# Reordering the head of a sliding-window attention and gated FFN kernel: first query halves of batch 0 ahead of the FFN, second halves between its first products

## The chip, the core and the metric

The kernel runs on one core of a Trainium2 chip. The metric is the device time of one execution in microseconds (us); the median of several executions counts. The engines are TensorE (PE in the profile; PEld is its weight load), VectorE (DVE), ScalarE (ACT), GpSimd (POOL) and SyncE (SP), which issues most DMA loads. An engine takes its instructions in the order of the program and waits where a value or a buffer is not ready.

## The reference

Causal attention with a window of 128 positions and 4 sink positions, 4 batches of 8 heads, 768 positions, head size 64; its output, with the heads joined to 512 columns, goes through a gated feed-forward network (FFN) with 1536 hidden columns. All inputs and outputs are float32.

```python
scores = scale * np.matmul(q, k.transpose(0, 1, 3, 2))
keep = is_sink | in_window            # pos < 4, or 0 <= query - key < 128
a = softmax(np.where(keep, scores, -1e9))
x = np.matmul(a, v).transpose(0, 2, 1, 3).reshape(B * S, H * D)
return (np.maximum(x @ w_gate, 0.0) * (x @ w_val)) @ w_out
```

## The kernel before

The order on every engine is written out by hand; nothing is rescheduled. Attention is done in units of two heads: a batch has four, U0 to U3 are batch 0, U4 to U7 batch 1 and so on. A unit passes through these steps, which the prediction calls by the names of the functions:

- `load_k`, `load_q` (L91 to L95), `load_v` (L97): DMA loads from SP. Keys and queries have three buffers each (`kf`, `qf`); values come for two units at once as seven loads (tiles 0 to 6, `vf`).
- `cast_kq` (L117) and `cast_v` (L106): POOL makes bf16 copies (`kn`, `qn`, `vn`).
- `T(u)` (L201): twelve PE transposes (L206); ACT copies the keys in five pieces (L211 to L216, `kE`), DVE copies the queries (L213, `qT`).
- `Sg(u, g)`, here S: scores for one of three groups of query columns (L229) and their exponential on ACT (L233, into `ee`). In the head a mask bias is first added on PE (L225); later DVE multiplies by a mask instead (L235).
- `V(u, part)`: products with the values and with ones (L247) for one half of the queries, 384 columns; then DVE normalises: a transpose (L253), a reciprocal (L254), a transpose (L255) and a product (L257) that writes this half of `xT`, the FFN's input. Part 0 needs score groups 0 and 1 and value tiles 0 to 3, part 1 groups 1 and 2 and tiles 2 to 6.

The FFN of a batch is `F1(b, g, m)`, for query half g and hidden column tile m of 12 (four gate products L273 over the four units of `xT`, ACT's relu L276, four value products L278, DVE's product L280 into `hT`), and `F2(b, t)`, six row tiles of the output (L289, L291, L292). F1 of half g needs that half of all four units. F1 and F2 take their PSUM banks in rotation from four (`G`), T, S and V from two pairs (`PP`); in the head T and V use `G` as well.

FFN weights are loaded in float32 by `load_w` (L124) into three buffers `ws` and cast on POOL by `cast_w` (L133): first column tiles 0 and 1, then 2 and 3, then 4 to 7 and 8 to 11, gate and value weights each in a buffer of its own. `load_wo` and `cast_wo` do the same for the output weights.

The head (L295 to L342) does all of batch 0's attention. After it come 18 slots per batch: 12 with two F1 each and 6 with one F2 each. `before` hangs loads and casts in front of a slot (L363 to L371 for the first batch), `after` hangs the 14 steps of the next batch's attention behind slots (`events`, `places`, L380 to L386). In slots 0 to 3 the first eight F1 are half 0 and half 1 of tiles 0 to 3.

Of the kernel before, what the change touches and what calls it, by code (L numbers as in the profile page):

```python
# [20 lines left out]
def kernel(  # L21
# [12 lines left out]
    nc = tc.nc  # L34
# [6 lines left out]
    KO = d_model // 128  # L41
# [49 lines left out]
    def load_k(u, eng=nc.sync):  # L91
        eng.dma_start(out=kf[u.i % NF][:], in_=k[u.b, 2 * u.p:2 * u.p + 2].rearrange("h (p n) d -> p h (n d)", n=NR))  # L92

    def load_q(u, eng=nc.sync):
        eng.dma_start(out=qf[u.i % NF][:], in_=q[u.b, 2 * u.p:2 * u.p + 2].rearrange("h (p n) d -> p h (n d)", n=NR))  # L95

    def load_v(w, tiles):  # L97
        dst = vf[w % NVF]
        b, h0 = w // 2, 4 * (w % 2)
        src = v[b, h0]  # L100
        for j in tiles:
            n = 128 if j < 6 else 14
            nc.sync.dma_start(out=dst[0:n, j, :, :],  # L103
                              in_=bass.AP(src.tensor, src.offset + ROWS[j] * D, [[D, n], [S * D, 4], [1, D]]))

    def cast_v(w, j0, j1):  # L106
        src, dst = vf[w % NVF], vn[w % NVN]
        nc.gpsimd.tensor_copy(dst[:, j0:j1, :, :].rearrange("p j h d -> p (j h d)"),  # L108
                              src[:, j0:j1, :, :].rearrange("p j h d -> p (j h d)"))
        for j in (1, 3, 5):  # L110
            if j0 <= j < j1:
                nc.gpsimd.tensor_copy(dst[0:4, j, :, :], src[0:4, 0, :, :])
# [8 lines left out]
    wsn = [0]  # L121
    staged = {}

    def load_w(m0, m1):  # L124
        for w, dst in ((moe_w_gate, wg), (moe_w_val, wv)):
            st = ws[wsn[0] % NW]
            wsn[0] += 1
            n = (m1 - m0) * 128
            nc.sync.dma_start(out=st[:, 0:KO * n].rearrange("p (k n) -> p k n", n=n),
                              in_=w.rearrange("(ko ki) n -> ki ko n", ki=128)[:, :, m0 * 128:m1 * 128])  # L130
            staged[m0, dst is wv] = st

    def cast_w(m0, m1):  # L133
        n = (m1 - m0) * 128
        for m in range(m0, m1):
            for x, dst in enumerate((wg, wv)):
                st = staged[m0, x == 1]
                o = (m - m0) * 128
                nc.gpsimd.tensor_copy(dst[:, :, m * 128:(m + 1) * 128],
                                      st[:, 0:KO * n].rearrange("p (k n) -> p k n", n=n)[:, :, o:o + 128])  # L140

    def load_wo(c):
        st = ws[wsn[0] % NW]
# [150 lines left out]
    with tc.manual_schedule():  # L294
        load_k(U[0])  # L295
        load_q(U[0], nc.scalar)
        setup()
        for u in (1, 2):
            load_k(U[u])
            load_q(U[u])  # L300
            if u == 1:
                load_v(0, (0, 1, 2, 3))
        load_v(0, (4, 5, 6))
        cast_kq(U[0])
        T(U[0])
        Sg(U[0], 0, bias=True)
        Sg(U[0], 1, bias=True)
        cast_kq(U[1])
        load_k(U[3])
        load_q(U[3])  # L310
        load_v(1, range(7))
        load_w(0, 2)
        T(U[1])
        Sg(U[0], 2, bias=True)
        cast_v(0, 0, 4)
        V(U[0], 0)
        Sg(U[1], 0, bias=True)
        cast_kq(U[2])
        cast_v(0, 4, 7)
        V(U[0], 1)  # L320
        Sg(U[1], 1, bias=True)
        T(U[2])
        Sg(U[1], 2, bias=True)
        V(U[1], 0)
        Sg(U[2], 0, bias=True)
        cast_kq(U[3])
        V(U[1], 1)
        Sg(U[2], 1, bias=True)
        T(U[3])
        Sg(U[2], 2, bias=True)  # L330
        cast_v(1, 0, 4)
        V(U[2], 0)
        Sg(U[3], 0, bias=True)
        cast_v(1, 4, 7)
        cast_w(0, 2)
        load_w(2, 4)
        V(U[2], 1)
        Sg(U[3], 1, bias=True)
        V(U[3], 0)
        Sg(U[3], 2, bias=True)  # L340
        V(U[3], 1)
        head[0] = False  # L342

        def kq_in(i):
            load_k(U[i])
            load_q(U[i])

        def events(i):

            a, c = U[i], U[i + 1]  # L350
            return [lambda: T(a), lambda: (Sg(a, 0), Sg(a, 1)), lambda: T(c), lambda: (Sg(a, 2), Sg(c, 0)),
                    lambda: (V(a, 0), V(a, 1)), lambda: (Sg(c, 1), Sg(c, 2)), lambda: (V(c, 0), V(c, 1))]

        ffn = [[lambda b=b, m=m: (F1(b, 0, m), F1(b, 1, m)) for m in range(FM)] +
               [lambda b=b, t=t: F2(b, t, b == B - 1 and t == 5) for t in range(6)] for b in range(B)]
        ffn[0][0:4] = [lambda: (F1(0, 0, 0), F1(0, 0, 1)), lambda: (F1(0, 0, 2), F1(0, 0, 3)),
                       lambda: (F1(0, 1, 0), F1(0, 1, 1)), lambda: (F1(0, 1, 2), F1(0, 1, 3))]
        before = {}

        def at(s, f):  # L360
            before.setdefault(s, []).append(f)

        at(0, lambda: (cast_w(2, 4), kq_in(4), load_w(4, 8)))  # L363
        at(1, lambda: (cast_kq(U[4]), kq_in(5), load_v(2, range(7))))
        at(2, lambda: cast_w(4, 8))
        at(3, lambda: load_w(8, 12))
        at(5, lambda: (cast_kq(U[5]), cast_v(2, 0, 7), kq_in(6), kq_in(7), load_v(3, range(7))))
        at(6, lambda: (cast_w(8, 12), load_wo(0), load_wo(1), load_wo(2)))
        at(9, lambda: (cast_kq(U[6])))
        at(10, lambda: (cast_v(3, 0, 7), [cast_wo(c) for c in range(3)]))  # L370
        at(12, lambda: (cast_kq(U[7]),))  # L371
        for b in (2, 3):
            s = 18 * (b - 1)
            i = NP * b
            at(s - 5, lambda i=i: (kq_in(i), kq_in(i + 1), load_v(i // 2, range(7))))
            at(s - 2, lambda i=i: (cast_kq(U[i]), kq_in(i + 2)))
            at(s + 1, lambda i=i: (cast_kq(U[i + 1]), cast_v(i // 2, 0, 7), kq_in(i + 3), load_v(i // 2 + 1, range(7))))
            at(s + 7, lambda i=i: (cast_kq(U[i + 2]), cast_v(i // 2 + 1, 0, 7)))
            at(s + 9, lambda i=i: (cast_kq(U[i + 3]),))
        after = {}  # L380
        for b in range(1, B):
            ev = events(NP * b) + events(NP * b + 2)
            places = [3, 4, 5, 6, 7, 8, 10, 11, 12, 13, 14, 15, 16, 17] if b == 1 else \
                     [0, 1, 2, 3, 5, 6, 7, 9, 10, 11, 12, 14, 15, 16]
            for p, f in zip(places, ev):
                after.setdefault(18 * (b - 1) + p, []).append(f)  # L386
        s = 0
        for b in range(B):
            for f in ffn[b]:
                for x in before.get(s, []):  # L390
                    x()
                f()
                for x in after.get(s, []):
                    x()
                s += 1
# [35 lines left out]
```

## Time and profile before

| what | value |
|---|---|
| median of 3 runs | 267.61 us (267.42 to 269.18) |
| the profiled execution | 267.93 us, span of its instructions 266.2 us |
| busy, share of the span | PE 247.5 us (93%), DVE 155.9 (59%), ACT 120.5 (45%), POOL 73.7 (28%) |
| chain that ended last | PE 73%, DVE 17% |
| DMA | 35.05 MB, mean 132 GB/s, nearly all of it on SP's queue |
| first F1 product | 31.20 us after the start |

The span runs from the first to the last instruction; the rest of the time lies around it. The busy share of PE counts a matmul from its issue, so waits inside a row are in it. The chain is followed back from the last instruction through whatever released each step. The page draws the span as 40 slices of 6.65 us, each digit the busy share in tenths.

### The profile page before, as it was taken

To read this page: it belongs to the slowest core of one execution; us is meant where nothing else is said; L and a number is where in the kernel's file an instruction comes from. 1 tells how busy PE (TensorE), PEld (TensorE's weight loads), DVE (VectorE), ACT (ScalarE), POOL (GpSimd) and SP (SyncE) were. 2 spreads that over 40 slices of the span, in tenths; PEclk is the share of its full clock that TensorE was granted. 3 is DMA by queue.
4 is the path that set the end of the run, shared out by engine and by line. 5 is a ranking of instruction groups with operands and counts; after the bars stand their busy time and mean duration, and the time that the engine had idled before them with its cause. 6 is when DMAs were issued, how large, how long until landed. Compare 5 with 4: busy or idle time off the path is not lost.

```text
span 266.2 us, 5290 instructions
## 1 busy us (share of the span) xinstructions
PE 247.5 (93%) x2073; PEld 145.3 (55%) x2084; DVE 155.9 (59%) x297; ACT 120.5 (45%) x250; POOL 73.7 (28%) x107
## 2 busy tenths in 40 slices
PE   1989699999999889999999999999999999999995
PEld 0445466656555456656655566566655456666443
DVE  4379744797836567698544566598543574444100
ACT  2757336744363437552661437743563423333221
POOL 6676448976523227000003523300000000000000
PEclk9999999999999999999999999999999999999999
DMA  6996999997079690000019956000003120000122
GB/s 233 287 270 205 354 311 281 368 277 273 2 221 285 212 236 2 1 2 0 2 46 293 309 182 126 0 2 1 0 2 118 42 79 0 2 1 0 42 97 100
DMA packets 44040, 35.05 MB, mean 132 GB/s; under 512 B 26992, under 2 KB 37488, under 8 KB 44016
## 3 DMA queue, kind: packets, MB, share of 16 engines
q1 hardware_dynamic: 43600, 34.20, 42.8%
q10 hardware_dynamic: 416, 0.52, 0.6%
q8 instruction: 16, 0.26, 0.4%
q14 instruction: 8, 0.07, 0.1%
HBM read 28.43 MB, written 6.29 MB: 130 GB/s over the span
## 4 chain that ended last, share of the span: by engine, by line
PE 73%; DVE 17%; SPq 3%; issue 2%; DMA 2%; ACT 1%; POOL 0%; DVEq 0%; POOLq 0%; ACTq 0%
PE g L289 21%; PE g L278 20%; PE g L273 20%; DVE R L255 5%; DVE t L253 5%; PE pp L247 4%; DVE xT L257 4%; PE pp L229 3%; PE pp L206 3%; DVE r L254 2%; DMA vf<-in_v_dram 2%; SPq L103 2%; DVE hT L280 1%; PE g L247 1%; SPq L92 1%
## 5 line engine op out<-in xcount | busy, mean ns | idle before, releaser
L273 PE MATMUL g<-xT,wg 128*128 128x384 bf16 x384 | 78.6, 326 | 2.0 <-DVE xT L257 1.3
L278 PE MATMUL g<-xT,wv 128*128 128x384 bf16 x384 | 78.1, 326 | 1.0 <-DVE hT L280 1.0
L280 DVE TENSOR_TENSOR hT<-gs,g 128x384 bf16<-128x384 f32 x96 | 51.1, 550 | 42.5 <-PE g L278 33.5
L276 ACT ACTIVATE gs<-g 128x384 f32<-128x384 f32 x96 | 46.3, 494 | 62.4 <-DVE hT L280 25.7
L289 PE MATMUL g<-wo,hT 128*128 128x512 bf16 (+1 forms) x289 | 63.6, 370 | 1.1 <-issue 0.8
L278 PEld LDWEIGHTS <-wv 128*128 128x128 bf16 x384 | 37.5, 98 | 28.0 <-issue 3.5
L273 PEld LDWEIGHTS <-wg 128*128 128x128 bf16 x384 | 35.7, 98 | 24.5 <-issue 2.3
L233 ACT ACTIVATE ee<-pp 128x1010 bf16<-128x1010 f32 (+2 forms) x48 | 44.4, 965 | 9.2 <-PE pp L229 9.2
L289 PEld LDWEIGHTS <-hT 128*128 128x128 bf16 x300 | 28.2, 98 | 30.5 <-issue 0.8
L235 DVE TENSOR_TENSOR ee<-ee,msk 128x1010 bf16<-128x1010 bf16 (+2 forms) x36 | 27.0, 756 | 17.4 <-ACT ee L233 16.8
L291 ACT COPY ot<-g 128x512 f32<-128x512 f32 (+1 forms) x24 | 13.9, 577 | 44.3 <-PE g L289 41.3
L115 POOL CAST kn<-kf 128x768 bf16<-128x768 f32 x16 | 13.6, 848 | 62.4 <-DMA kf<-in_k_dram 48.7
L253 DVE STREAM_TRANSPOSE t<-pp 128x384 f32<-128x384 f32 x24 | 13.8, 577 | 13.1 <-PE pp L247 12.5
L255 DVE STREAM_TRANSPOSE R<-r 128x384 f32<-128x384 f32 x32 | 18.5, 578 | 1.1
L108 POOL CAST vn<-vf 128x1792 bf16<-128x1792 f32 (+2 forms) x10 | 14.3, 1425 | 16.7 <-DMA vf<-in_v_dram 16.7
L229 PE MATMUL pp<-qT,kE 64*128 64x255 bf16 (+4 forms) x224 | 16.4, 252 | 2.6 <-DVE xT L257 2.4
L247 PEld LDWEIGHTS <-vn 128*64 128x64 bf16 x288 | 12.5, 109 | 9.2 <-issue 6.9
L229 PEld LDWEIGHTS <-kE 64*128 64x128 bf16 x224 | 8.1, 94 | 15.9 <-issue 11.9
L213 DVE COPY qT<-pp 128x768 bf16<-128x768 bf16 x12 | 11.5, 957 | 6.6 <-ACT kE L212 6.6
L115 POOL CAST qn<-qf 128x768 bf16<-128x768 f32 x16 | 13.7, 859 | 2.1 <-DMA qf<-in_q_dram 2.1
L257 DVE TENSOR_TENSOR xT<-pp,R 128x384 bf16<-128x384 f32 x24 | 13.4, 557 | 0.8
L247 PEld LDWEIGHTS <-ones 128*64 128x64 bf16 x288 | 12.5, 111 | 0.0
(55 smaller groups left out, 156.0 us busy)
## 6 DMA issues: line engine op xcount, KB each, us to landing
kf<-in_k_dram SPq DMA_DIRECT2D x16, 384.0 KB, 4.9
vf<-in_v_dram SPq DMA_DIRECT2D x48, 128.0 KB, 5.4
out_dram<-ot SPq DMA_DIRECT2D x23, 256.0 KB, 2.0
qf<-in_q_dram SPq DMA_DIRECT2D x15, 384.0 KB, 5.1
ws<-in_moe_w_out_dram SPq DMA_DIRECT2D x3, 1024.0 KB
ws<-in_moe_w_gate_dram SPq DMA_DIRECT2D x2, 1024.0 KB, 5.9
ws<-in_moe_w_val_dram SPq DMA_DIRECT2D x2, 1024.0 KB, 8.0
ws<-in_moe_w_gate_dram SPq DMA_DIRECT2D x2, 512.0 KB, 5.8
```

Source lines behind the costliest of these rows:

```text
L115: copy(dst[:], src[:].rearrange("p h (n d) -> p n h d", d=64))
L229: nc.tensor.matmul(out=ps[:, h, c0:c1], lhsT=kE[t][64 * h:64 * h + 64, x0:x0 + 128], rhs=qT[t][64 * h:64 * h + 64, q0:q0 + c1 - c0], start ...
L233: nc.scalar.activation(x, ps[:, :, 0:n], Act.Exp, bias=0.0, scale=scale)
L235: nc.vector.tensor_tensor(x, x, msk[:, g, 0:n].unsqueeze(1).to_broadcast([128, 2, n]), op=Alu.mult)
L247: nc.tensor.matmul(out=(pv, pd)[which][64 * h:64 * h + 64, o0:o0 + c1 - c0], lhsT=lhs, rhs=ee[u.i % NE][:, g, h, c0:c1], start=i == 0, sto ...
L253: nc.vector.transpose(out=t1[:], in_=pd[:, 0:CUT])
L255: nc.vector.transpose(out=R[:].rearrange("p (c e) -> p c e", e=32), in_=r[:].unsqueeze(2).to_broadcast([128, CUT // 32, 32]))
L273: nc.tensor.matmul(out=gp[:, 0:n], lhsT=wg[:, ko, m * 128:(m + 1) * 128], rhs=x[:, ko, c], start=ko == 0, stop=ko == KO - 1)
L276: nc.scalar.activation(gs[:, 0:n], gp[:, 0:n], Act.Relu, bias=0.0, scale=1.0)
L278: nc.tensor.matmul(out=vp[:, 0:n], lhsT=wv[:, ko, m * 128:(m + 1) * 128], rhs=x[:, ko, c], start=ko == 0, stop=ko == KO - 1)
L280: nc.vector.tensor_tensor(hT[:, m, c], gs[:, 0:n], vp[:, 0:n], op=Alu.mult)
L289: nc.tensor.matmul(out=op[:, 0:c1 - c0], lhsT=hT[:, m, t * 128:(t + 1) * 128], rhs=wo[:, m, c0:c1], start=m == 0, stop=m == FM - 1)
```

## The change

In the head only the first query halves of batch 0 are finished: the order on PE becomes T and two score groups for each unit with V of part 0 behind, and groups 2 of U0 and U1. Groups 2 of U2 and U3 and the four V of part 1 go between the first F1. The first sixteen F1 are now half 0 of tiles 0 to 7 and then half 1 of tiles 0 to 7, two to a slot. Weights come in six pairs of column tiles, gate and value of a pair in one buffer. Value tiles 4 to 6 are loaded and cast behind the first pair of weights. Loads and casts are hung on other slots, and the last eight of batch 1's fourteen attention steps move one slot ahead (the first six stay).

```diff
+    def load_w(i):
+        st = ws[wsn[0] % NW]
+        wsn[0] += 1
+        for x, w in enumerate((moe_w_gate, moe_w_val)):
+            nc.sync.dma_start(out=st[:, 1024 * x:1024 * x + 1024].rearrange("p (k n) -> p k n", n=256),
+                              in_=w.rearrange("(ko ki) n -> ki ko n", ki=128)[:, :, i * 256:(i + 1) * 256])
+        staged[i] = st
...
-        for u in (1, 2):
-            load_k(U[u])
-            load_q(U[u])
-            if u == 1:
-                load_v(0, (0, 1, 2, 3))
-        load_v(0, (4, 5, 6))
+        load_k(U[1])
+        load_q(U[1])
+        load_v(0, (0, 1, 2, 3))
+        load_k(U[2])
+        load_q(U[2])
         cast_kq(U[0])
         T(U[0])
         Sg(U[0], 0, bias=True)
         Sg(U[0], 1, bias=True)
         cast_kq(U[1])
         load_k(U[3])
         load_q(U[3])
-        load_v(1, range(7))
-        load_w(0, 2)
+        load_v(1, (0, 1, 2, 3))
+        load_w(0)
+        load_v(0, (4, 5, 6))
+        load_v(1, (4, 5, 6))
+        load_w(1)
+        load_w(2)
         T(U[1])
+        Sg(U[1], 0, bias=True)
+        cast_v(0, 0, 4)
+        Sg(U[1], 1, bias=True)
+        cast_kq(U[2])
+        V(U[0], 0)
+        T(U[2])
+        Sg(U[2], 0, bias=True)
+        Sg(U[2], 1, bias=True)
+        cast_kq(U[3])
+        V(U[1], 0)
         Sg(U[0], 2, bias=True)
-        cast_v(0, 0, 4)
-        V(U[0], 0)
...
+        T(U[3])
+        Sg(U[3], 0, bias=True)
+        cast_v(1, 0, 4)
+        cast_w(0)
+        Sg(U[3], 1, bias=True)
+        V(U[2], 0)
+        Sg(U[1], 2, bias=True)
+        V(U[3], 0)
         cast_v(0, 4, 7)
...
         cast_v(1, 4, 7)
-        cast_w(0, 2)
-        load_w(2, 4)
...
+        cast_w(1)
+        load_w(3)
         head[0] = False
...
+        ffn[0][0:8] = [lambda g=g, m=m, x=x: (F1(0, g, m), [f() for f in x], F1(0, g, m + 1)) for g, m, x in (
+            (0, 0, [lambda: Sg(U[2], 2, bias=True), lambda: V(U[0], 1)]),
+            (0, 2, [lambda: Sg(U[3], 2, bias=True), lambda: V(U[1], 1)]),
+            (0, 4, [lambda: V(U[2], 1), lambda: V(U[3], 1)]),
+            (0, 6, []), (1, 0, []), (1, 2, []), (1, 4, []), (1, 6, []))]
...
-        at(0, lambda: (cast_w(2, 4), kq_in(4), load_w(4, 8)))
-        at(1, lambda: (cast_kq(U[4]), kq_in(5), load_v(2, range(7))))
-        at(2, lambda: cast_w(4, 8))
-        at(3, lambda: load_w(8, 12))
-        at(5, lambda: (cast_kq(U[5]), cast_v(2, 0, 7), kq_in(6), kq_in(7), load_v(3, range(7))))
-        at(6, lambda: (cast_w(8, 12), load_wo(0), load_wo(1), load_wo(2)))
-        at(9, lambda: (cast_kq(U[6])))
-        at(10, lambda: (cast_v(3, 0, 7), [cast_wo(c) for c in range(3)]))
-        at(12, lambda: (cast_kq(U[7]),))
+        at(0, lambda: (cast_w(2), load_w(4), kq_in(4)))
+        at(1, lambda: (load_w(5), kq_in(5), load_v(2, range(7))))
+        at(2, lambda: (cast_w(3), cast_kq(U[4])))
+        at(3, lambda: (cast_w(4), load_wo(0)))
+        at(4, lambda: (cast_kq(U[5]), kq_in(6), kq_in(7), load_v(3, range(7))))
+        at(5, lambda: cast_v(2, 0, 7))
+        at(6, lambda: (cast_w(5), load_wo(1), load_wo(2)))
+        at(8, lambda: (cast_kq(U[6])))
+        at(9, lambda: (cast_v(3, 0, 7), [cast_wo(c) for c in range(3)]))
+        at(11, lambda: (cast_kq(U[7]),))
...
-            places = [3, 4, 5, 6, 7, 8, 10, 11, 12, 13, 14, 15, 16, 17] if b == 1 else \
+            places = [3, 4, 5, 6, 7, 8, 9, 10, 11, 12, 13, 14, 15, 16] if b == 1 else \
```

## The prediction

> **What bounds the kernel now.** I read the page first, then the chain that ended last in order of time, then the timeline of the first 45 us, and the two-microsecond windows for the DMA rate. The page's slices say where TensorE (PE) is not full and where DMA is:
>
> ```profile
> PE   1989699999999889999999999999999999999995
> DMA  6996999997079690000019956000003120000122
> ```
>
> One slice is 6.65 us. From the sixth slice on PE shows nines with a few eights; the first five (to about 31 us) are the head, the attention of batch 0, and only there can an order of work free much PE time. In the head DMA is also near full. The chain, in order of time (start, length, what):
>
> ```profile
> 15.95 0.59 DVE t L253
> ...
> 17.52 0.56 DVE xT L257
> 18.07 0.86 DVE qT L213
> ...
> 31.20 0.81 PE g L273 x4
> ...
> 41.76 0.67 PE pp L206 x12
> ```
>
> The head is no queue of PE work: its chain goes through the normalisation on VectorE (DVE: L253, L254, L255, L257) and through the copy of transposed queries (qT) that stands behind it. FFN products begin at 31.20 and run on PE without a break to T(U4), whose first matmul the timeline has at 41.59. Head work on PE is 18.7 us by the rows below (four units of 4.68), and 25.3 us pass between the first transpose at 5.93 and 31.20. The timeline gives the durations:
>
> ```profile
> 6.70 0.82 PE L206 MATMUL g<-ident,qn 128*128 128x128 bf16 x6
> ...
> 10.39 0.51 PE L206 MATMUL g<-ident,kn 128*128 128x128 bf16 x6
> ...
> 12.25 0.24 ACT L216 COPY kE<-kE 128x12 bf16<-128x12 bf16 x1
> ...
> 23.07 0.62 POOL L139 CAST wv<-ws 128x512 bf16<-128x512 f32 x1 [0.99 <-DMA ws<-in_moe_w_val_dram]
> ```
>
> Six transposes take 0.82 us at first and 0.51 later; T(U1)'s keys, transposed from 10.39, are usable only after ScalarE (ACT) ends its five copies at 12.49; the first `wv` tiles are there at 23.0, eight microseconds before use. The second place is the border between batches:
>
> ```profile
> 76.39 0.67 PE pp L206 x12
> ...
> 96.54 0.67 PE pp L206 x12
> ...
> 133.96 0.67 PE pp L206 x12
> ...
> 157.64 0.67 PE pp L206 x12
> ```
>
> These are T(U7) and T(U8), then T(U11) and T(U12). Between the first two lie 20.15 us with 17.8 us of PE work: four F2 of 2.65 (24 matmuls took 5.29), two F1 of 1.30, T 0.67, two score groups of 0.52, two V pairs of 1.45; 2.3 us are idle, because V(U7) ends slot 17 and the next batch's first F1 waits for its normalisation. Between the second two lie 23.68 us with 23.1 us of work (six F2, the rest alike): 0.6 us idle.
>
> **The change, part by part: the head.** Per-step durations, all from the head's timeline rows: T 0.66 on PE; S of groups 0 and 1, bias 0.54 then scores 0.32; S of group 2, 0.45 and 0.28; V part 0 0.74, part 1 0.83; exp starts 0.43 after the scores and takes 1.02 (0.89 for group 2); T's five key copies 1.08 on ACT; a normalisation 2.05 on DVE, a second one queued behind it 1.96 later; qT copy 0.95; F1 1.30, its `hT` product 0.55. Up to T(U1) nothing differs. Then, engine by engine in the new order:
>
> ```
> S1.0 scores 12.53   key copies of T1 end 12.49; bias was done 11.6: 0.9 idle
> S1.1, V0.0  12.85 to 14.45;  T2 14.45 to 15.11
> DVE         V0.0 normalised 14.57 to 16.62, then qT of T2 to 17.48
> S2.0 scores 17.52   bias was done 15.65: 1.9 idle
> S2.1, V1.0, S0.2    to 20.16;  T3 to 20.82
> DVE         V1.0 normalised 19.56 to 21.61, then qT of T3 to 22.47
> S3.0 scores 22.51   bias was done 21.36: 1.15 idle
> S3.1, V2.0, S1.2, V3.0   to 25.89
> DVE         V2.0 normalised to 26.60, V3.0 from 26.51 to 28.57
> F1(0,0,0)   three gate products at 27.13 (bank read by L253), the fourth
>             at 28.6 (needs xT of U3): 1.2 and 1.0 idle; ends 29.42
> S2.2 30.14, V0.1 30.97, F1 m1 32.27, F1 m2 33.57, S3.2 34.29, V1.1 35.12,
> F1 m3 36.42, F1 m4 37.72, V2.1 38.55, V3.1 39.38, F1 m5 40.68, F1 m6 41.98 (ends)
> DVE         V2.1, V3.1 normalised 38.63 to 42.65, only then hT of m5 to 43.12
> F1 m7       val half waits for that bank: 42.63 to 43.14; ends 43.79 = T(U4)
> ```
>
> The same work lies ahead of T(U4) in both kernels (four units and eight F1), so the head term is 43.79 - 41.59 = +2.2 us. FFN does start earlier (28.4 if its early products are counted against 31.20), but 4.8 us of attention are still to do, and waits are opened: today T(u) is followed by work of another unit while its copies run, in the changed order by its own scores; and the last V in front is directly followed by the product that needs it, where today V(U3,1) lies between. Each of five waits rests on rows good to some 0.2 us: +1.2 to +3.2.
>
> **What is costed at nothing, and its cover.** In SP's queue the 14 `vf` loads become 4 + 4 in front and 3 + 3 behind the first weights; weights become twelve loads of 512 KB instead of four of 512 KB and four of 1 MB, four more issues of about 0.4 us on an engine with nothing else to do. In the built program each SP load also waits until the one eight places before it has landed; at the landings below that lets every load out 3 us or more before its turn. Latest landings, from today's rows: pair 0 no later than today's 23.0 (fewer bytes ahead of it), six `vf` loads 0.55 MB at the 289 GB/s of 20 to 22 us: 24.9, then 1.05 MB a pair at the 350 GB/s of 26 to 28 us: 27.9, 30.9, 33.9. GpSimd (POOL) casts a pair in four steps of 0.56, and stands behind two V casts (1.2 us each): ready by 25.4, 30.2, 33.2, 36.2, needed at 27.1, 32.3, 36.4, 40.7. Cover is 1.7 us at least; once it is gone each microsecond late is one microsecond. The wait for a free buffer moves also: pair 3 takes pair 0's buffer and stands on SP ahead of U4's loads; these land by 39.1 behind pair 4, are cast by 40.7, and T(U4) wants them at 43.8. U5 and `vf` of batch 1 are needed 6 and 13 us later still. Second-half `vn` tiles are cast by about 27, wanted at 30.1.
>
> The Trainium skill speaks against the smaller loads: DMA: Bandwidth & Descriptors, Rules for kernel authors, asks for 1 MiB per DMA or more. Its fit of 2.0 us plus bytes over 436 GB/s per DMA would make a pair 6.4 us if nothing overlapped, pair 3 ready at about 46 and the sum some 6 us larger (an estimate from that page). Today's rows have several loads in flight and 350 GB/s, so I keep nothing.
>
> **Slots of batch 1.** The first six events keep their slots; the last eight go one slot earlier. V(U5) comes two slots behind V(U4) instead of three. In the later batches it already does: T(U9) at 103.06 to T(U10) at 127.44 holds 1.6 us idle, T(U5) at 48.27 to T(U6) at 69.89 holds 1.4: +0.2, bounds -0.2 (DVE has room) and +0.6 (one more `hT` late by 0.55). V(U7) moves to slot 16, as in the later batches: 2.3 - 0.6 = -1.7, bounds -1.3 and -2.1. U6's and U7's loads keep their order and the `wo` casts still precede slot 12.
>
> **Sum.** +2.2 + 0.2 - 1.7 = +0.7 on the profiled execution's 267.93 (span 266.2 and 1.7 around it), 268.6. That execution is 0.3 above the median of the runs, 267.61, so the forecast for the median is 268.3; with the terms' bounds -1.1 to +2.5, 266.5 to 270.1.
>
> **Rivals.**
> The head costs nothing. If DVE took qT ahead of the normalisation's end, the waits at 17.5 and 22.5 would shrink by 0.9 and 0.3, and if the first F1 found U3's values 1 us sooner the head would be level: -1.5, so 266.1. For it: of the 25.3 us of today's head 6.6 are idle and could be won. Against: the built program's order has each qT behind the normalisation on DVE, which takes one instruction after the other.
>
> PE slows down in the new gaps (this one is slower). The rows show slow transposes, 0.82 for 0.51, until about 10 us, with the profile's granted clock full throughout, and quick ones after gaps of up to 0.9 us. If a gap of 1.9 us, or the 2.2 of 25.9 to 28.6 with its short work between, brings that back for the 4 us it lasted from 5.93, 2 us of work are lost: 270.3, and 272.3 if twice. It decides from the first gap above 0.9 us that is followed by slow matmuls.
> On this the Trainium skill (TensorE: Matmul & The Clock Gate, part 1) says that the clock falls to half after an idle window of about 3.4 us; by that rule no gap here is long enough and the sum is unchanged.
>
> Weights late. If the loads of 512 KB run at the 213 GB/s that 16 to 18 us shows, a pair takes 4.9 us, pair 3 lands at 39.6, is ready at 41.9 and the seventh F1 ends 1.2 us late: 269.5; with pair 2 and POOL late as well, 271.
>
> The border is not healed. If V(U7) in slot 16 is still late because DVE lags, the -1.7 is lost: 270.0.
>
> **How the numbers follow.** Forecast 0.50, head level 0.16, PE slow 0.16, weights late 0.08, border 0.10. A change of 1% (2.7 us) is about what a measurement of this kernel can tell from none: below 264.9 lies 0.06 (of the second case, if more of the idle 6.6 us is filled), above 270.3 lie 0.06, 0.10, 0.04 and 0.04 of the others, 0.24; 0.70 within. The range reaches down to the level head and up past one slow spell: 266.0 to 271.2; the likeliest case's own is 266.5 to 270.1.
>
> **What will show it.** Right: scores L229 near 17.5 and 22.5 behind qT, the first FFN product near 27 to 28.6, T(U4) near 43.8, no POOL cast of weights that PE waits for, T(U7) to T(U8) with under 1 us idle. Wrong: T(U4) before 42 (head), L273 rows of more than 0.2 us a matmul after 28 us (clock), PE released by L138 casts (weights), or a chain through DVE at the start of batch 1.

## The result

The changed kernel takes 270.99 us (median of 20 runs, 267.94 to 273.56), the kernel before 267.71 (20 runs, 267.31 to 269.61). The ratio is 1.0096, with an interval of 1.0076 to 1.0115: slower by one per cent. The forecast was 268.3 with a range of 266.0 to 271.2. So the range held, but the likeliest case's own range, 266.5 to 270.1, did not, and the median lies above 270.3, for which the prediction had given a chance of 0.24. (Medians are over all runs; the ratio leaves out runs over 1.5% above the fastest of their kernel, four of the 20 here.)

The profiled execution took 270.69 us, 269.0 of it the span. First its page, the slices that were shown of before:

```profile
PE   0877899997999999999999999999999999999995
DMA  6999998981019957000009958000002220000123
```

Three things differ from the page of before. PE's first five slices are 0, 8, 7, 7, 8 where they were 1, 9, 8, 9, 6: the head has more idle PE time than before. And a 7 stands in the tenth slice (60.5 to 67.3 us), in batch 1, where nothing but nines and eights stood. DMA has 1, 0, 1 in the tenth to twelfth slice where it had 7, 0, 7: batch 1's loads are done earlier. Now the gaps of the head, from the timeline of PE (start, length, engine, line, what; in brackets the idle time ahead and what ended it):

```profile
17.72 0.40 PE L229 MATMUL pp<-qT,kE 64*128 64x253 bf16 x4 [1.90 <-DVE qT L213]
...
22.71 0.39 PE L229 MATMUL pp<-qT,kE 64*128 64x253 bf16 x4 [1.08 <-DVE qT L213]
...
27.32 0.65 PE L273 MATMUL g<-xT,wg 128*128 128x384 bf16 x3 [1.20 <-DVE t L253]
28.86 0.32 PE L273 MATMUL g<-xT,wg 128*128 128x384 bf16 x1 [0.89 <-DVE xT L257]
```

These are four of the waits in the prediction's walk, released by the instructions it named, each 0.2 to 0.3 us later than it put them. The chain in order of time has T(U4), T(U7) and T(U8) at

```profile
44.38 0.67 PE pp L206 x12
...
78.26 0.67 PE pp L206 x12
...
99.36 0.67 PE pp L206 x12
```

With the first matmul of T(U4) at 44.22 (before: 41.59), the first F2 at 75.50 (70.40) and T(U8) at 99.20 (96.38), the 2.8 us between the two spans split into three. In this kernel one score pair of U6 (0.54 us) stands ahead of the first F2 instead of behind it, and is taken out of the second and third term:

| stretch | predicted | measured in the profile |
|---|---|---|
| head, to T(U4) | +2.2 | 44.22 - 41.59 = +2.6 |
| T(U4) to the first F2 | +0.2 | 31.28 - 0.54 - 28.81 = +1.9 |
| first F2 to T(U8), the border | -1.7 | 23.70 + 0.54 - 25.98 = -1.7 |
| T(U8) to the end | 0 | 169.8 - 169.8 = 0 |

The second row is where this profile went wrong. It is seen on three engines at once, in the timeline from 58 us:

```profile
59.02 5.95 POOL L152 CAST wo<-ws 128x1024 bf16<-128x1024 f32 x6
64.93 0.82 POOL L115 CAST kn<-kf 128x768 bf16<-128x768 f32 x1
65.70 0.82 POOL L115 CAST qn<-qf 128x768 bf16<-128x768 f32 x1
```

```profile
62.89 1.01 DVE L280 TENSOR_TENSOR hT<-gs,g 128x384 bf16<-128x384 f32 x2
63.81 3.74 DVE L235 TENSOR_TENSOR ee<-ee,msk 128x1014 bf16<-128x1014 bf16 x2
```

```profile
63.02 0.36 PE L229 MATMUL pp<-qT,kE 64*128 64x255 bf16 x6 [1.16 <-DVE xT L257]
67.11 0.25 PE L247 MATMUL pp<-ee,vn 128*64 128x134 bf16 x3 [0.69 <-DVE ee L235]
72.92 0.81 PE L278 MATMUL g<-xT,wv 128*128 128x384 bf16 x4 [0.47 <-DVE hT L280]
```

L235 multiplies the scores of a group by the mask; both operands lie in SBUF. Two such products take 1.27 us together where no cast runs (the last experiment); here they take 3.74, the first alone 3.25. GpSimd runs eight casts without a pause from 59.02 to 66.5, and the first product ends 0.54 us behind the last of them, its own length. The last three rows are PE's waits in this stretch, 2.32 us together; the kernel before has one there, of 0.62. The second is V(U5), waiting for the long product. The first, 1.16, is behind the normalisation of V(U4), which stands on DVE behind another mask product, U5's first, and that took 1.82 beside the `v` casts (55.91 to 59.07). In the experiments below, as long as the product ahead of it on DVE keeps its 0.59, this wait goes with the length of U5's first product: 0.35 or 0.36 where that takes 0.69, 1.08 at 1.76 and 1.30 at 1.98. The products of `hT` (L280, one operand in PSUM) under the same casts take what they always take, 0.55 us each (0.54 to 0.56 over the whole run). In the kernel before the `wo` loads landed later and the casts waited for them in between (three pauses), and its longest mask product is 1.42 us.

### The profile page after: what moved, and what is told of

The parts are those of the page before. It is cut to its first block, busy times and chain, and to the rows that moved or that the text cites. A ratio compares the mean times of both kernels' runs of the same rounds, so it can differ in the third digit from the quotient of the medians.

```text
span 269.0 us, 5302 instructions
## 1 busy us (share of the span) xinstructions
PE 247.6 (92%) x2084; PEld 145.2 (54%) x2084; DVE 159.6 (59%) x297; ACT 120.2 (45%) x250; POOL 72.0 (27%) x107
## 4 chain that ended last, share of the span: by engine, by line
PE 74%; DVE 19%; issue 2%; DMA 2%; ACT 1%; POOL 0%; DVEq 0%; ACTq 0%
PE g L289 21%; PE g L278 20%; PE g L273 19%; DVE R L255 5%; DVE t L253 5%; PE pp L229 4%; DVE xT L257 4%; PE pp L247 4%; PE pp L206 3%; DVE r L254 2%; DVE hT L280 2%; DMA kf<-in_k_dram 2%; DVE qT L213 1%; PE pp L225 1%; PE g L247 1%
## 5 line engine op out<-in xcount | busy, mean ns | idle before, releaser
L278 PE MATMUL g<-xT,wv 128*128 128x384 bf16 x384 | 78.1, 326 | 1.9 <-DVE hT L280 1.9
L280 DVE TENSOR_TENSOR hT<-gs,g 128x384 bf16<-128x384 f32 x96 | 50.9, 550 | 40.5 <-PE g L278 30.4
L276 ACT ACTIVATE gs<-g 128x384 f32<-128x384 f32 x96 | 46.2, 494 | 60.5 <-PE g L273 26.7
L289 PE MATMUL g<-wo,hT 128*128 128x512 bf16 (+1 forms) x300 | 65.1, 371 | 0.0
L278 PEld LDWEIGHTS <-wv 128*128 128x128 bf16 x384 | 37.5, 98 | 28.5 <-issue 2.8
L235 DVE TENSOR_TENSOR ee<-ee,msk 128x1010 bf16<-128x1010 bf16 (+2 forms) x36 | 31.3, 877 | 15.2 <-ACT ee L233 14.7
L253 DVE STREAM_TRANSPOSE t<-pp 128x384 f32<-128x384 f32 x28 | 16.2, 578 | 12.2 <-PE pp L247 11.8
L257 DVE TENSOR_TENSOR xT<-pp,R 128x384 bf16<-128x384 f32 x28 | 15.6, 558 | 1.0
L247 PE MATMUL pp<-ee,vn 128*64 128x255 bf16 (+8 forms) x256 | 14.2, 236 | 0.7 <-DVE ee L235 0.7
```

Of the source, the lines that this page charges most:

```text
L235: nc.vector.tensor_tensor(x, x, msk[:, g, 0:n].unsqueeze(1).to_broadcast([128, 2, n]), op=Alu.mult)
L247: nc.tensor.matmul(out=(pv, pd)[which][64 * h:64 * h + 64, o0:o0 + c1 - c0], lhsT=lhs, rhs=ee[u.i % NE][:, g, h, c0:c1], start=i == 0, sto ...
L253: nc.vector.transpose(out=t1[:], in_=pd[:, 0:CUT])
L276: nc.scalar.activation(gs[:, 0:n], gp[:, 0:n], Act.Relu, bias=0.0, scale=1.0)
L278: nc.tensor.matmul(out=vp[:, 0:n], lhsT=wv[:, ko, m * 128:(m + 1) * 128], rhs=x[:, ko, c], start=ko == 0, stop=ko == KO - 1)
L280: nc.vector.tensor_tensor(hT[:, m, c], gs[:, 0:n], vp[:, 0:n], op=Alu.mult)
```

## The experiments

A second thing is not in this profile. Each run comes with the mean clock that was granted to PE. Of the 20 runs of the changed kernel, 13 have a mean below 0.997, mostly 0.993 or 0.994, of the kernel before 2 of 76. The median of the 7 others is 269.44, of the 13 it is 271.05. None of the low runs of this kernel has a profile. So two theories were on the table for the missing 2.7 us: the mask products behind rows of casts, and a clock that falls after a gap of the new head. The prediction's other rivals are excluded by the profile: no PE wait is released by a cast of weights, the border gained its 1.7.

**The new places of batch 1 alone.**

```diff
 (the kernel before)
-            places = [3, 4, 5, 6, 7, 8, 10, 11, 12, 13, 14, 15, 16, 17] if b == 1 else \
+            places = [3, 4, 5, 6, 7, 8, 9, 10, 11, 12, 13, 14, 15, 16] if b == 1 else \
```

> The kernel before with one part of the change alone: the last eight attention steps of batch 1 one slot earlier. Theory (border): V(U7) in slot 16 leaves its normalisation covered, so T(U7) to T(U8) has under 1 us idle; 1.7 us gained there, and V(U5) two slots behind V(U4) costs 0.2: about 266.1 us, ratio 0.994. Rival (the step that was mis-sized is the slot move itself: masks and two normalisations of V(U4) and V(U5) crowd on VectorE whatever GpSimd does): 1.8 us are lost between T(U5) and the first F2, 267.7, ratio 1.000.

Measured 265.78 us (265.48 to 266.41), ratio 0.9934 (0.9920 to 0.9949). First F2 to T(U8) gained 1.74, T(U4) to the first F2 lost 0.44: the border's term and the slots' term, each within the bounds of the prediction. So the 1.9 of the changed kernel is not the two-slot distance of V(U5) from V(U4); that costs 0.4.

**T ahead of V.**

```diff
-        V(U[0], 0)
         T(U[2])
+        V(U[0], 0)
...
-        V(U[1], 0)
-        Sg(U[0], 2, bias=True)
         T(U[3])
+        V(U[1], 0)
+        Sg(U[0], 2, bias=True)
```

> The changed kernel with T(U2) ahead of V(U0,0) and T(U3) ahead of V(U1,0), nothing else. Theory (the head's loss is the copy of the queries behind the normalisation on VectorE): the scores of U2 start at 16.3 instead of 17.7 and those of U3 at 20.1 to 20.4 instead of 22.7, the first FFN product 2.2 us sooner, T(U4) near 42.1: 268.7 us, ratio to before 1.004. Rival (the head is paced by loads, casts or ScalarE): T(U4) stays near 44.3 and the time at 271, ratio 1.010 to 1.012.

Measured 267.07 (266.04 to 268.09), ratio 0.9979 (0.9963 to 0.9995); T(U4) at 42.26, 1.96 earlier than in the changed kernel, as expected. The qT copies are ahead of the normalisations on DVE, and the waits of 1.90 and 1.08 are gone. The time fell by twice as much as T(U4) did: one run of 12, not 13 of 20, had a clock below 0.997, and in the profile of this kernel the longest mask product of U4 and U5 was 1.64 and T(U4) to the first F2 29.51 (31.28 in the changed kernel). It gained from both other causes too.

**The `wo` casts held.** GpSimd copies two elements of U5's last masked group ahead of the last two `wo` casts, so they can't start before that product is done; one cast goes ahead of the `v` casts.

```diff
-        at(9, lambda: (cast_v(3, 0, 7), [cast_wo(c) for c in range(3)]))
+        at(8, lambda: (cast_wo(0), cast_v(3, 0, 7)))
+        at(9, lambda: (gp_copy(held[:], ee[U[5].i % NE][:, 2, 1, 405:407]), cast_wo(1), cast_wo(2)))
```

> The changed kernel with the output weights' casts kept off the mask products of batch 1: the first third is cast ahead of the value cast, the other two wait on GpSimd for the mask product of U5's last group (a copy of two elements reads it). Theory (a mask product, two operands in SBUF, is shut out while GpSimd runs its casts back to back): the mask product of 3.25 us falls to about 0.7, the wait of PE ahead of V(U5) goes, 1.5 to 1.9 us are gained: 269.2 us, ratio 1.004, and the runs lie closer together than 267.9 to 273.6. Rival (VectorE is simply crowded because V(U5) follows V(U4) sooner): nothing gained, 271, ratio 1.010.

Measured 269.93 (268.26 to 271.09), ratio 1.0086 (1.0056 to 1.0116). In its profile U5's products take 0.68 and 0.58 and T(U4) to the first F2 takes 29.69 instead of 31.28, the 1.6 that was expected. The median is only 1.1 lower, and runs with the same clock hardly differ: the three at full clock have a median of 269.26 (269.44 in the changed kernel), the three others 270.93 (271.05). So the hold shows what made that product long; that it wins time is not shown, and 270.99 may come from runs with a shorter product than the profiled one. Half of the runs had the low clock, the profiled one among them, and there it can be seen. Windows of this kernel, then one of the T-first kernel and of the changed kernel (stretch, its length, busy time and instructions of PE, PEld, DVE, ACT, POOL, then the granted clock and DMA):

```profile
15.62:19.03 3.41, 1.52 (x17) 0.80 (x15) 2.63 (x5) 1.35 (x7) 2.39 (x5) 1.00 1.06 323
19.03:22.44 3.41, 3.41 (x28) 1.53 (x28) 0.85 (x3) 1.92 (x2) 2.99 (x6) 0.50 1.13 264
22.44:25.85 3.41, 2.69 (x32) 1.30 (x30) 1.96 (x3) 2.66 (x7) 2.11 (x4) 1.00 0.82 256
```

```profile
24.55:27.96 3.41, 1.70 (x10) 0.87 (x9) 2.20 (x5) 0.49 (x1) 2.44 (x5) 1.00 0.96 309
27.96:31.37 3.41, 3.41 (x41) 2.27 (x40) 2.43 (x6) 1.35 (x2) 2.60 (x5) 1.00 1.09 384
```

```profile
26.83:30.24 3.41, 2.03 (x14) 0.99 (x15) 2.10 (x5) 0.49 (x1) 2.68 (x6) 1.00 1.06 365
```

The clock changes only at multiples of 3.41 us from one another, on a grid whose place differs from run to run. The window with the 1.89 us gap (1.52 busy) is followed by exactly one window at 0.50; the windows with 1.70 and 2.03 busy are followed by full clock.

**The gap ahead of the first FFN product filled.**

```diff
         V(U[3], 0)
...
+        Sg(U[2], 2, bias=True)
+        V(U[0], 1)
         head[0] = False
...
-            (0, 0, [lambda: Sg(U[2], 2, bias=True), lambda: V(U[0], 1)]),
+            (0, 0, []),
```

> The changed kernel with S(U2,2) and V(U0,1) moved from behind the first F1 to ahead of it, into the wait for the last normalisation. Theory (the 2.2 us in which PE waits between V(U3,0) and the fourth product of the first F1 is a loss of order alone): 1.55 us of PE work go into it, 1.2 to 1.5 us gained: 269.6 us, ratio 1.007. Rival (VectorE is what ends last there; one more normalisation ahead of hT gives the wait back at the next bank): at most 0.3 gained, 270.7, ratio 1.009.

Measured 268.63 (266.19 to 271.1), ratio 1.0001 (0.9970 to 1.0032); T(U4) 42.97, 1.25 earlier. Seven of 12 runs still have the low clock (268.35 to 271.1); the other five take 266.19 to 267.34. So the spell does not need the gap that was filled; the longest one left is that of 1.90 us.

**All three edits at once.** T first, filled gap and held casts, as above.

> The changed kernel with three edits at once: T(U2) ahead of V(U0,0) and T(U3) ahead of V(U1,0); S(U2,2) and V(U0,1) ahead of the first FFN product; two of the wo casts held until U5's last masked group, and one put ahead of batch 1's v casts. Theory (three separate losses: the gaps behind qT, the gap ahead of the first FFN product, the mask products that lie under the casts): T(U4) near 41.0 (44.22 less the 1.96 and the 1.25 that the two head edits gave alone), T(U4) to the first F2 29.5 to 30.0, time 264.5 to 265.5, under the 265.8 of the new places alone. Rival (the edits fill the same gap, or take the same loss away): no better than the 267.1 of the best of them.

Measured 266.72 (264.45 to 267.15), ratio 0.9936 (0.9907 to 0.9965). No run of 8 had the low clock, but the expected 264.5 to 265.5 was met in two runs only. In the profile T(U4) is at 40.96, as expected, but T(U4) to the first F2 takes 31.20, not 29.5 to 30.0: the `wo` cast that had been put in front now meets U4, and a product of U4 takes 3.12 us under it. Earlier work of PE had moved the products, and the cast that was harmless in one kernel was in the way in the next.

**The gaps of the head kept warm.**

```diff
-            for h in range(2):
+            for h in list(range(2)) * (1 + again):
...
-        Sg(U[2], 0, bias=True)
+        Sg(U[2], 0, bias=True, again=3)
...
-        Sg(U[3], 0, bias=True)
+        Sg(U[3], 0, bias=True, again=2)
```

> The changed kernel with the two bias matmuls of S(U2,0) issued four times and those of S(U3,0) three times (the same values written again, 1.6 and 1.1 us more of PE work inside the gaps of 1.90 and 1.08 us), nothing else. Theory (the long gap in front lets PE's clock fall for some microseconds in part of the executions): no matmul moves in the profile, T(U4) stays near 44.2, but no execution has the spell, the runs lie closer together, and the median falls from 271.0 to 269 to 269.7, with the mask products still long in some. Rival (the clock spells come from elsewhere, or the median of 271 is the mask products' alone): 270.5 to 271.3 with the same spread; 271.5 if the added matmuls delay the scores.

Measured 270.47 (267.94 to 274.2), ratio 1.0075 (1.0046 to 1.0104): the median missed the expectation and lies by the rival's 270.5, and 4 of 12 runs, the profiled one among them, had a low clock. The profile says where:

```profile
26.54:29.95 3.41, 1.32 (x19) 0.94 (x18) 3.12 (x7) 0.85 (x1) 2.73 (x5) 1.00 1.05 349
29.95:33.37 3.42, 3.42 (x21) 1.68 (x22) 0.56 (x1) 0.96 (x2) 3.03 (x7) 0.50 1.05 370
...
64.08:67.50 3.42, 1.63 (x17) 1.04 (x17) 3.32 (x8) 1.75 (x2) 3.42 (x5) 1.00 0.01 5
67.50:70.91 3.41, 3.41 (x12) 1.47 (x10) 2.83 (x3) 1.06 (x3) 1.33 (x2) 0.50 0.00 0
```

```profile
30.22 1.49 PE L278 MATMUL g<-xT,wv 128*128 128x384 bf16 x4
...
34.53 0.81 PE L278 MATMUL g<-xT,wv 128*128 128x384 bf16 x4
```

The gap of 1.90 no longer does it. The two gaps of 1.20 and 0.89 ahead of the first FFN product do, together: no single one is long, but one window holds both. The second spell follows on the mask products: two of them take 3.44 us together beside casts (from 58.03), V(U4)'s normalisation is late behind them, PE waits 1.56 us for it (to 66.36), and that window has 1.63 us of work. So here the lock-out sets off the clock. The four products of L278 take 1.49 in the spell, 0.81 outside.

**Warm and held.** The two edits before, together.

> The changed kernel with the repeated bias matmuls and with the held wo casts. If the forecast missed only these two things, this is the kernel that it described: 267.8 to 268.6, runs within about 0.7 us of each other, T(U4) near 44.1 and T(U4) to the first F2 near 29.7. If one of the two is not the cause, its part stays: 269.3 to 270 (the held casts alone gave 269.9).

Measured 270.0 (268.99 to 271.84), ratio 1.0093 (1.0062 to 1.0124), low clock in 2 of 6. The expectation failed, for reasons that the profile shows: the FFN gap is still there (spell from 30.22 to 33.64), and the `wo` cast in front meets the first product of U4, which takes 2.72.

**The `wo` casts cut into pieces.**

```diff
-        for i in range(2):
-            nc.gpsimd.tensor_copy(wo[:, 4 * c + 2 * i:4 * c + 2 * i + 2, :].rearrange("p k n -> p (k n)"),
-                                  st[:, 1024 * i:1024 * i + 1024])
+        for i in range(8):
+            nc.gpsimd.tensor_copy(wo[:, 4 * c + i // 2, 256 * (i % 2):256 * (i % 2) + 256],
+                                  st[:, 256 * i:256 * i + 256])
```

> The changed kernel with each wo cast of 1024 columns cut into four of 256 (24 casts instead of 6, the same elements), nothing else. If a VectorE product with two SBUF operands waits for the end of the one GpSimd cast that runs when it starts, no mask product lasts over 1.3 us, and some 1.5 us are won: 269.3. If it waits for a whole row of casts that stand back to back, the longest stays near 3 us, the casts take longer by their own fixed parts, and the time is 271 or more.

```profile
60.69 7.46 POOL L152 CAST wo<-ws 128x256 bf16<-128x256 f32 x19
```

```profile
63.75 1.38 DVE L235 TENSOR_TENSOR ee<-ee,msk 128x1014 bf16<-128x1014 bf16 x2
```

The two products lie in the middle of a row of short casts and take 1.38 together: no long wait here. The others, under `v` casts that were not cut, still take up to 2.20. The time is 273.52 (269.27 to 275.81), ratio 1.0103 (1.0051 to 1.0155). The profiled run and one other come to 269.3 and 269.4, as the first theory said. Three have a clock of 0.987 or 0.988, which two spells would give (the warm kernel's 0.987 had two); the sixth, 272.87 at full clock, is unexplained. As an edit it loses.

**The filled kernel with one bias pair repeated.** `again=1` for S(U2,0), and the fill: the gap of 1.90 is shortened by the 0.54 us of one pair and not closed.

> The filled kernel (S(U2,2) and V(U0,1) ahead of the first FFN product) with the two bias matmuls of S(U2,0) issued twice: 0.54 us of PE work more, so its gap of 1.90 us becomes 1.36 us and is not closed. Theory (PE's clock is set in windows of 3.41 us, and a window in which PE is idle for 1.8 us or more is followed by one at half speed): with the gap of 1.36 no window reaches 1.8 us, so none of the runs has a granted clock under 0.997, where 7 of 12 of the filled kernel had one, and the median falls from 268.6 to 266.8, the level of its undisturbed runs (266.2 to 267.3). Rival (any gap over about a microsecond can do it, or the spells are chance): a third or more of the runs still show 0.992 to 0.994, median 268 to 269.

Measured 268.05 (266.82 to 271.86), ratio 1.0019 (0.9984 to 1.0055). In the profile the gap is 1.47, in a window with no more idle time than that. One run of 12 had the low clock, where 7 of 12 had it: with a gap of 1.47 instead of 1.90 most of the spells are gone. Six runs are at 266.8 to 267.3, the expected level; five more are at 268.8 to 270.3 at full clock. These have no profile; a long mask product would fit, but it is not shown.

**All edits, and three holds on GpSimd.**

```diff
-        at(3, lambda: (cast_w(4), load_wo(0)))
+        at(3, lambda: load_wo(0))
...
-        at(5, lambda: cast_v(2, 0, 7))
+        at(5, lambda: (gp_copy(held[:, 0:2], ee[U[4].i % NE][:, 1, 1, 505:507]), cast_v(2, 0, 7), cast_w(4)))
...
-        at(9, lambda: (cast_v(3, 0, 7), [cast_wo(c) for c in range(3)]))
+        at(8, lambda: (gp_copy(held[:, 2:4], ee[U[5].i % NE][:, 0, 1, 503:505]), cast_v(3, 0, 7), cast_wo(0)))
+        at(9, lambda: (gp_copy(held[:, 4:6], ee[U[5].i % NE][:, 2, 1, 405:407]), cast_wo(1), cast_wo(2)))
```

> T(U2) and T(U3) ahead of the V, the filled gap, and three holds on GpSimd's queue by copies of two elements: batch 1's first v casts and the casts of the fifth weight pair wait for U4's second masked group, the second v casts and the first wo cast for U5's first group, the last two wo casts for U5's third. Theory (mask products under rows of dense casts are what was left): no product of U4 or U5 over 1.4 us, T(U4) to the first F2 30.2 or less, no clock spells, 264.0 to 264.8, the lowest of all. Rival (a hold makes something else late: vn for V(U4), weights for the ninth F1, or wo for the first F2): PE waits for a POOL cast there, 266 to 268.

Measured 269.28 (267.58 to 269.98), ratio 1.0046 (1.0022 to 1.0069). The holds moved `v`, weight and k/q casts into one row and put that row on U4's third product:

```profile
50.96 0.60 POOL L139 CAST wg<-ws 128x512 bf16<-128x512 f32 x1
...
53.72 0.60 POOL L139 CAST wv<-ws 128x512 bf16<-128x512 f32 x1
54.27 0.82 POOL L116 CAST kn<-kf 128x768 bf16<-128x768 f32 x1
55.04 1.17 POOL L116 CAST qn<-qf 128x768 bf16<-128x768 f32 x1
```

```profile
51.48 5.28 DVE L236 TENSOR_TENSOR ee<-ee,msk 128x814 bf16<-128x814 bf16 x2
```

```profile
55.59 0.36 PE L248 MATMUL pp<-ee,vn 128*64 128x255 bf16 x5 [1.21 <-DVE ee L236]
```

The first of the two products takes 4.05 us, the longest seen, and gets in only as the seventh cast ends, counted from the one that runs when it starts (50.96) to that of `kn`. That a product waits for one cast is thus too little, and it is not only the wide `wo` casts that do it. Yet such a row does not always shut a product out. The kernel with the new places alone has the same weight casts, back to back from 50.34 to 56.65, and the same product in their midst:

```profile
52.02 0.61 POOL L139 CAST wg<-ws 128x512 bf16<-128x512 f32 x1
52.57 0.97 POOL L139 CAST wv<-ws 128x512 bf16<-128x512 f32 x1
53.49 1.06 POOL L139 CAST wg<-ws 128x512 bf16<-128x512 f32 x1
```

```profile
52.49 0.59 DVE L235 TENSOR_TENSOR ee<-ee,msk 128x814 bf16<-128x814 bf16 x1
```

It takes 0.59, and the one behind it 0.69; there it is the casts beside them that are longer, 0.97 and 1.06 instead of 0.61. Eight of 12 runs have the low clock. The profiled one has not; the waits of PE behind the product (1.21 and 1.56 us) are the likely place, as the next experiment's profile has it there. The rival of the expectation did not come true (no PE wait behind a cast); the kernel was slower by the very mechanism it was to remove.

**The changed order with shorter gaps and the same holds.** One bias pair again, five gate products of the first F1 issued once more, and the holds of the run before.

```diff
-        for ko in range(KO):
+        for ko, end in [(0, 0), (1, 0), (2, 0), (1, 0), (2, 1)] * ((b, g, m) == (0, 0, 0)) + [(0, 0), (1, 0), (2, 0), (3, 1)]:
```

> The changed kernel, its order unchanged, with the two gaps shortened by repeated work and the same three holds on GpSimd: the bias matmuls of S(U2,0) twice (gap 1.90 to 1.36 us), and five gate products of the first F1 issued once more ahead of its four (gap 0.89 to about 0.1; they write what the four then write again). If lock-out and clock spells are all that the forecast missed, this runs as forecast: 267.7 to 268.7, no run with a granted clock under 0.997, the spread not over 1.6 us (the kernel before: 266.95 to 268.49), T(U4) 44.2 to 45.2. If a term of the head or of the slots was also wrong: 269.5 or more without any spell.

Measured 274.12 (272.1 to 274.27), ratio 1.0217 (1.0181 to 1.0254). T(U4) is at 45.06 and the head has no spell; but the holds bring their 4.06 us product here too, and in the profile the clock is halved from 67.27 to 70.69, after a window with 1.53 us of work that holds the 1.56 us wait behind that product (5 of 6 runs have the low clock). It was to be the kernel of the forecast, and because of these holds it says nothing on that.

**The holds put right.** T first, filled gap, and every row of casts placed where no mask product of U4 or U5 is due: the fifth weight pair back in its old place, the first `v` casts behind U4's second product, the sixth pair behind U5's first, `wo` behind U5's third, the second `v` casts behind U7's.

```diff
-        at(5, lambda: cast_v(2, 0, 7))
-        at(6, lambda: (cast_w(5), load_wo(1), load_wo(2)))
+        at(5, lambda: (gp_copy(held[:, 0:2], ee[U[4].i % NE][:, 1, 1, 505:507]), cast_v(2, 0, 7)))
+        at(7, lambda: (gp_copy(held[:, 2:4], ee[U[5].i % NE][:, 0, 1, 503:505]), cast_w(5), load_wo(1), load_wo(2)))
...
-        at(9, lambda: (cast_v(3, 0, 7), [cast_wo(c) for c in range(3)]))
-        at(11, lambda: (cast_kq(U[7]),))
+        at(9, lambda: (gp_copy(held[:, 4:6], ee[U[5].i % NE][:, 2, 1, 405:407]), [cast_wo(c) for c in range(3)]))
+        at(11, lambda: (cast_kq(U[7]), cast_v(3, 0, 7)))
```

> T(U2) and T(U3) ahead of the V, the filled gap, and the holds of the run before put right: the fifth weight pair is cast where the changed kernel casts it (a pause of GpSimd ahead of U5's casts), the first v casts of batch 1 wait for U4's second masked group, the sixth weight pair for U5's first, the three wo casts for U5's third, and the second v casts come behind U7's. Theory (a VectorE product with two SBUF operands is shut out for as long as a row of casts stands back to back, and a window of 3.41 us with 1.8 us idle halves the next): no mask product of U4 or U5 over 1.2 us, T(U4) to the first F2 near 29.0 (the one-pair kernel: 28.96), no run with a granted clock under 0.997, T(U4) 40.0 to 41.0 by the start of the clock's windows, 263.6 to 264.8: faster than the new places alone (265.8). Rival (the casts held back come too late instead): PE waits behind a POOL cast, wo for the first F2 or the sixth pair for the eleventh F1, 265.5 to 267.

Measured 264.24 (263.78 to 264.91), ratio 0.9861 (0.9827 to 0.9895), the fastest of all, under both kernels and under the new places alone.

```profile
60.04 0.18 POOL L375 COPY held<-ee 128x2 bf16<-128x2 bf16 x1 [3.38 <-DVE ee L236]
60.16 3.97 POOL L153 CAST wo<-ws 128x1024 bf16<-128x1024 f32 x4
```

```profile
51.07 0.59 DVE L236 TENSOR_TENSOR ee<-ee,msk 128x814 bf16<-128x814 bf16 x1
...
58.70 1.27 DVE L236 TENSOR_TENSOR ee<-ee,msk 128x1014 bf16<-128x1014 bf16 x2
```

The product that took 4.05 takes 0.59, the pair that took 3.74 takes 1.27. T(U4) is at 39.90, T(U4) to the first F2 is 28.97 (31.28 in the changed kernel), all six runs have the clock at 1.0, and they lie within 1.2 us. Between this kernel and the one of the first holds, the head and the PE order are the same; only where GpSimd's casts stand differs (and, with them, the issue of two `wo` loads), and that is worth 5.0 us, the clock's part included, and 3.8 against the four runs of that kernel at full clock (median 268.1).

## Why the prediction was right in part, and where it failed

The range held because it had been drawn up past one slow spell of the clock; the case that was called likeliest did not come. The head and the border are right by their mechanism, two other steps are wrong.

**The head's walk held.** Scores at 17.72 and 22.71 (17.52 and 22.51 predicted), the first FFN product at 27.32 (27.13), the fourth at 28.86 (28.6), T(U4) at 44.22 (43.79). T(U0) itself started 0.48 later in this execution (6.41 against 5.93), of which 0.1 was left at T(U1). The rival of a level head is refuted.

**The border held**: -1.7 in the changed kernel and -1.74 in the kernel with the new places alone. Weights were never late. (The fit that the prediction quotes against the smaller loads is given, on the page that it names, for DMAs issued from GpSimd; these are issued from SP.)

**"Slots of batch 1", +0.2 with a bound of +0.6, was mis-sized**: 1.9 in the profile, of which the new distance costs 0.4 (the first experiment). The step that failed is the one ahead of it, "what is costed at nothing". There GpSimd's casts were priced by when their results were wanted, with a cover of 1.7 us at least, and that cover was there. What a row of casts does to another engine while it runs was not asked. The trace of before had a hint: L235 there took up to 1.42 beside casts and 0.59 to 0.69 elsewhere. The Trainium skill has the rule (SBUF — State Buffer, on the two separate sides): a VectorE instruction with two SBUF inputs and a GpSimd instruction that reads SBUF lock each other out, the later one for the whole instruction of the other. The runs agree on who is hit (L235; L280 with an operand in PSUM is not) but not on how long: one `wo` cast is 1.0 us and the waits were 2.6 (3.25 less 0.69) and 3.5 us.

**The clock was the rival given 0.16, and the one that most runs show.** Its price was right (2 us; 271.05 - 269.44 = 1.6, and half of a window of 3.41 is 1.7), and its 270.3 is 0.7 under the median. What failed was the sentence set against it, that "no gap here is long enough". The Trainium skill (TensorE: Matmul & The Clock Gate, part 1) gives a free-running window of 3413 ns, which the 3.41 us between the clock's steps confirm; the prediction read its "idle window" as a gap of that length. It also took the clock of before for full throughout; the granted clock is on record there from 10.0 us only, and the slow transposes lie ahead of that. The runs show that the window need only be about half idle. In all profiles, behind the start, windows with 1.32, 1.33, 1.52, 1.53 and 1.63 us of PE work (1.78 idle and more) were followed by half the clock, those with 1.70 (1.71 idle) and more were not. (One window with 1.55 in the tail of the new-places kernel was not either; 12 of its 300 F2 records are missing there.) The prediction's own sentence, that 2.2 us were lost between 25.9 and 28.6 "with its short work between", named the right thing to add up.

With that rule a profile gives an estimate of how many runs will be hit, by sliding the grid of 3.41 us over its PE idle time and counting the positions at which a window has 1.8 us idle (an estimate; the grid's place is taken as even):

| kernel | share of positions | runs below 0.997 |
|---|---|---|
| before | 0 | 2 of 76 |
| changed | 0.57 | 13 of 20 |
| new places alone | 0 | 0 of 6 |
| T first | 0.37 | 1 of 12 |
| filled | 0.50 | 7 of 12 |
| all three edits | 0 | 0 of 8 |
| `wo` casts held | 0.87 | 3 of 6 |
| warm | 0.37 | 4 of 12 |
| warm and held | 0.37 | 2 of 6 |
| `wo` casts cut | 0.58 | 3 of 6 |
| filled, one pair | 0 | 1 of 12 |
| first holds | 0.38 | 8 of 12 |
| shorter gaps, first holds | 0.38 | 5 of 6 |
| holds put right | 0 | 0 of 6 |

T first, the `wo` casts held and the two kernels with the first holds do not fit well; one profile need not stand for all runs, and four of these profiles hold a spell themselves, which moves what comes after it. With 1.75 instead of 1.8 the warm kernel's share is 0.64, and the others rise by 0.06 at most. What the table does tell apart is none from some.

So of the 2.7 us between 268.3 and 270.99, the clock accounts for about 1.6 in the median run, since 13 of 20 have the spell. The rest is put down to the mask products: among the seven runs without the spell, four take 267.94 to 269.44, around the forecast, and three 270.69 to 271.26, the profiled one with its 3.25 us product among these. That the other two had such a product is likely, not shown. How often it comes can't be told from one profile. No run takes both causes out of the changed order and leaves the rest: of the two kernels meant for that, each put casts on another product. That 268.3 would be met without them is therefore argued from the parts; the kernel with the holds put right, which has neither cause, has another head.

**What stays open**: what lets a mask product in between casts. It waited 3.5 us through casts of 0.60 us that stood back to back, and not at all among the same casts in the kernel with the new places alone, nor in a row of 0.39 us casts. The 273.5 of the kernel with the cut casts, and the five runs of the one-pair kernel at 268.8 to 270.3, are not accounted for either.

## What to carry to other kernels

Price a moved GpSimd cast twice: by when its result is needed, and by which VectorE instructions with two SBUF operands fall due while the row of casts runs. A cast that is held back by copying two elements of the product it must not meet costs 0.2 us and is sure not to run under that product, though it can land under the next one (the first holds); a cast put by slot number can move onto another product whenever PE's work moves. Add up PE's idle time over windows of 3.41 us, not gap by gap: at some 1.8 us in one window the next 1.7 us are at stake, in a share of the runs that a single profile gives roughly. In the filled kernel 0.54 us of repeated matmuls in the gap took the low clock from 7 of 12 runs to 1.

## What the hardware showed that was not expected

A VectorE product of 0.59 us took 4.05 us under a row of GpSimd casts of which none is longer than 1.2 us, while products with a PSUM operand kept their 0.55 us; among the same casts in another kernel it took 0.59. PE's clock halves for exactly one window of 3.41 us after a window with 1.52 us of work, and not after one with 1.70; since the grid of windows stands elsewhere in each run, the same kernel has the spell in one run and not in the next. And the two are coupled: a wait of PE that goes back to locked-out products lowered the clock in its turn (64.08 to 70.91 in the warm kernel).
